# Two layers of sliding-window attention and a one-row MLP: the last MLP started before the last tile is done, a shorter path to the first scores, and a new order of the instructions

## The chip, the core and the metric

The kernel runs on one core of a Trainium2 chip. The core has five engines that run their own instruction streams and meet through semaphores: TensorE (PE; its weight loads are listed as PEld), VectorE (DVE), ScalarE (ACT), GpSimd (POOL) and SyncE (SP), which mostly issues transfers. The metric is device time in microseconds (us), the median of several runs.

## What is computed

```python
def _A_ref(x, wqkv, wo):                    # attention
    H = 32; Dh = D // H; W = 256
    q, k, v = split(x @ wqkv)
    scores = einsum("bhqd,bhkd->bhqk", q, k) * (Dh ** -0.5)
    mask = (i - j >= 0) & (i - j < W)       # the last 256 positions
    p = softmax(where(mask, scores, -1e9))
    return einsum("bhqk,bhkd->bhqd", p, v) @ wo

def _B_ref(x, w_r, w_gate, w_up, w_down):   # MLP of one row
    r = x @ w_r
    idx = argsort(-r)[:, :1]                # the one best row
    x_sel = x[idx]
    y = (silu(x_sel @ w_gate) * (x_sel @ w_up)) @ w_down
    return x + scatter(y * sigmoid(r[idx]), idx)

x = A_x                                     # 2048 rows of 512, bf16
for layer in range(2):
    x = x + _A_ref(layernorm(x), A_wqkv, A_wo)
    x = x + _B_ref(layernorm(x), w_r, w_gate, w_up, w_down)
```

There are 32 heads of 16 columns, 2048 rows, 512 columns and an MLP width of 1792. In each layer the MLP is applied to a single row: the one with the best score `r` of all 2048.

## The kernel before

**Tiles and steps.** The rows are cut into 16 tiles of 128. A tile passes through `ln_tile` (line 735: statistics on DVE, the inverse root and the normalisation on POOL, a transpose), `proj` (line 771: the projections of Q, K and V), `attend` (line 1298) and `out_tile` with `mod_tile` (lines 834 and 851: output projection, residual, statistics, the row score `r`, and the second normalised sum). In the second layer `mod_tile` also sends the finished tile to DRAM (line 884). Attention of a tile is cut into steps (`step`, line 1182): scores into two PSUM banks (line 1231), one exponential on ACT (line 1244), a mask on POOL (line 1250), products with V in bank 6 (line 1274). Tile 0 has 4 steps, tile 1 has 8, all others 9; three pairs of score banks are used in turn, and three steps are bound together as a visit (`VISIT = 3`, `S.bind`, with a slack `P_LEAD`).

**V's way.** V is stored to DRAM and read back in another layout (`vstore`, lines 1284 and 1287, SP's queue) before products can use it. K is copied four times under a mask into `KT` (line 802, "kbd").

**One projection bank.** Bank 7 (`BK_PR`) is shared by Q, K and V of all tiles but the first, by the output projections, and by the first layer's MLP. A use of it is a transaction: from its first matmul to its eviction no other use may enter.

**The MLP.** `mod_global(L)` (line 901) reduces the scores to the best one, finds the row's tile, picks the tile (ACT, line 941), gathers the row through matmuls with a one-hot vector (lines 955 and 957), multiplies by gate and up (line 980), applies the gate function, multiplies by down (line 1017 in the first layer, 1035 in the second). In the first layer all matmuls use bank 7, and the row is updated in place (line 1028). Tiles 0 to 4 of the second layer do not wait for that: they start with the row not updated, and if the best row lies in those five tiles, they are replayed from copies in DRAM. In the second layer the MLP stands at the very end: its row is written over the stored output by a 1 KB transfer (`fix`, line 1044).

**The check.** `check` (line 1314) reduces the reciprocals of all softmax sums to a flag. At the end all engines read the flag (line 1549) and branch (1550): to "pass", or to "safe", a slow general version of the whole kernel.

**What sets the order.** Nothing is ordered by hand. Every operation is given reads, writes, an estimated duration and a priority. A planner in the kernel's program simulates the five engines and gives each free engine the ready operation of lowest priority number; the resulting five lists are the instruction streams, with waits derived from the reads and writes. One tile is one unit of priority (1e6). Offsets per kind of work are named constants:

```python
1077     P_STEP = 1.453
1081     P_LN = -2.934
1082     P_PRJ = -1.175
1083     P_FIN = 1.042
1084     P_MG = 0.121
1344             S.prio_base = (n + self.P_PRJ) * ST
1364                 S.prio_base = (n + self.P_MG) * ST
1371         S.prio_base = (K + 4) * ST
1372         self.check()
1373         self.mod_global(1)
1374         self.warm(self.warmn[1])
```

`n` counts tiles over both layers, `K` is 32. In `proj` the constants `P_Q`, `P_K` and `P_V` are added, and for the first tile the three follow each other by these as well. `warm` adds matmuls whose results nobody reads, with the lowest priority of all: 21 at the start (line 699), 40 at the end (line 1295).

## Time and profile before

| | |
|---|---|
| median of 3 runs | 388.71 us (387.01 to 391.85) |
| the profiled execution | 390.14 us, its span 388.4 us |
| instructions in the span | 17651 |
| granted TensorE clock, mean | 0.954 |
| busy: PE, DVE, ACT, POOL | 346.4, 268.0, 264.9, 266.3 us |
| moved by DMA | 31.23 MB, 80 GB/s |

A line of the timeline gives the start, the duration of the whole group, the engine, the source line, the operation, what it writes and reads, how many such instructions are merged, and in brackets the idle time before it with what ended it. A line of the chain gives start, duration and what ran. A line of a stretch gives its bounds, its length, the busy time and count of PE, PEld, DVE, ACT and POOL, then the granted TensorE clock, the DMA share and GB/s. Where a stretch was asked for one source line, only that line's engine is counted. A line for one source line gives the engine, the operation, the count, the shortest, median and longest duration in ns, and the first and last start; a q behind an engine's name is its sequencer.

### The profile page before, as it was taken

Reading aid. Unit: us, or ns where it says so; the run is one execution under the profiler, and the core shown is the slowest. Engines: PE = TensorE matmul, PEld = TensorE weight load, DVE = VectorE, ACT = ScalarE, POOL = GpSimd, SP = SyncE. Lnnn points to the kernel's source line nnn. Section 1 sums busy time; section 2 is a strip of 40 time slices with the busy share of each in tenths; the row PEclk is TensorE's granted clock in tenths of the full one; section 3 lists DMA queues with packets and bytes.
Section 4 is the critical chain, followed back from the end, with each engine's and each line's share of the span. In section 5 each row is a group of like instructions: output and inputs, shape, how many; then the busy total and the mean of one; then the engine's idle time right before and its main releaser. Section 6 shows DMA issues by size and latency. Waiting matters only on the chain.

```text
span 388.4 us, 17651 instructions
## 1 busy us (share of the span) xinstructions
PE 346.4 (89%) x7793; PEld 277.5 (71%) x7793; DVE 268.0 (69%) x695; ACT 264.9 (68%) x284; POOL 266.3 (69%) x475
## 2 busy tenths in 40 slices
PE   6788989998999999998879798999999999997970
PEld 2567778777888888886657467788888888886470
DVE  6868967777777667677764487977666667775820
ACT  1078788887888888884945058788888888886010
POOL 6779968877888888775734069888888776665400
PEclk9789999999999999999998869999999999999975
DMA  8744567656444465553430222434433333221000
GB/s 265 219 64 66 88 136 119 110 113 99 99 101 98 93 99 102 99 100 71 58 44 15 44 20 72 57 73 73 73 73 73 73 71 73 59 59 29 26 8 5
DMA packets 72723, 31.23 MB, mean 80 GB/s; under 512 B 52672, under 2 KB 72000, under 8 KB 72640
## 3 DMA queue, kind: packets, MB, share of 16 engines
q1 hardware_dynamic: 70384, 27.81, 37.4%
q10 hardware_dynamic: 2256, 2.23, 1.8%
q8 instruction: 62, 1.02, 1.2%
q14 instruction: 21, 0.17, 0.2%
HBM read 14.29 MB, written 7.87 MB: 57 GB/s over the span
## 4 chain that ended last, share of the span: by engine, by line
PE 65%; DVE 15%; POOL 9%; DMA 3%; issue 3%; ACT 2%; DVEq 0%; ACTq 0%; POOLq 0%
PE f_PS L1274 20%; PE f_PS L1231 15%; PE f_PS L781 11%; PE f_PS L843 7%; PE f_PS L812 6%; DVE f_KT L802 3%; DMA f_OT<-f_ONORM 2%; PE f_PS L1295 2%; POOL f_PT L1250 2%; DVE f_ST L741 2%; ACT f_PT L1244 1%; DVE f_VN L815 1%; POOL f_xres L867 1%; POOL f_XN L749 1%; DVE f_QT L1109 1%
## 5 line engine op out<-in xcount | busy, mean ns | idle before, releaser
L1244 ACT ACTIVATE f_PT<-f_PS 128x1024 bf16<-128x1024 f32 x276 | 261.6, 1025 | 85.0 <-PE f_PS L1231 60.9
L1250 POOL TENSOR_TENSOR f_PT<-f_PT,f_TM 128x384 bf16<-128x384 bf16 x128 | 127.7, 999 | 53.3 <-ACT f_PT L1244 51.7
L1274 PE MATMUL f_PS<-f_VBD,f_PT 128*128 128x68 bf16 x2880 | 115.5, 198 | 7.6 <-DVE f_ONORM L830 4.6
L1274 PEld LDWEIGHTS f_PS<-f_VBD,f_PT 128*128 128x128 bf16 x2880 | 105.2, 98 | 22.5 <-issue 12.1
L1231 PE MATMUL f_PS<-f_QT,f_KT 64*128 64x128 bf16 (+3 forms) x2976 | 89.3, 205 | 9.8 <-DVE f_QT L1109 5.8
L1231 PEld LDWEIGHTS f_PS<-f_QT,f_KT 64*128 64x128 bf16 x2976 | 72.7, 95 | 29.3 <-issue 14.7
L781 PE MATMUL f_PS<-f_XNT,f_wqkv 128*128 128x128 bf16 x1024 | 70.7, 225 | 5.6 <-DVE f_GWR L928 2.1
L781 PEld LDWEIGHTS f_PS<-f_XNT,f_wqkv 128*128 128x128 bf16 x1024 | 60.5, 100 | 10.2 <-DVE f_KTN L799 2.6
L802 DVE TENSOR_SCALAR f_KT<-f_KTN,f_KM 128x512 bf16<-128x512 bf16 x128 | 47.8, 434 | 0.9
L843 PE MATMUL f_PS<-f_wo,f_OT 128*128 128x512 bf16 x128 | 34.8, 396 | 2.5 <-DMA f_OT<-f_ONORM 1.8
L812 PE MATMUL f_PS<-f_wqkv,f_XNT 128*128 128x512 bf16 x128 | 34.0, 389 | 0.5 <-DVE f_MV L742 0.5
L1109 DVE CAST f_QT<-f_PS 128x512 bf16<-128x512 f32 x32 | 21.9, 685 | 10.7 <-PE f_PS L781 10.3
L830 DVE TENSOR_TENSOR f_ONORM<-f_PS,f_RDA 128x256 bf16<-128x256 f32 x64 | 27.1, 423 | 2.0
L828 DVE RECIPROCAL f_RDA<-f_PS 128x16 f32<-128x16 f32 x64 | 16.2, 254 | 17.3 <-PE f_PS L1274 16.9
L799 DVE CAST f_KTN<-f_PS 128x512 bf16<-128x512 f32 x32 | 22.1, 690 | 7.1 <-PE f_PS L781 7.1
L1229 PE MATMUL f_PS<-f_BM,f_II 64*128 64x64 bf16 (+1 forms) x256 | 25.4, 192 | 0.0
L815 DVE CAST f_VN<-f_PS 128x512 bf16<-128x512 f32 x32 | 22.2, 693 | 4.6 <-PE f_PS L812 3.4
L847 DVE TENSOR_TENSOR f_xres<-f_PS,f_xin 128x512 f32<-128x512 f32 x16 | 11.1, 692 | 19.4 <-PE f_PS L843 19.4
L858 DVE BATCH_NORM_STATS2 f_ST<-f_xres 128x6 f32<-128x512 f32 x32 | 22.2, 692 | 1.0
L847 DVE TENSOR_TENSOR f_xres<-f_PS,f_xres 128x512 f32<-128x512 f32 x16 | 11.0, 691 | 16.8 <-PE f_PS L843 16.8
L860 DVE SCALAR_TENSOR_TENSOR f_JUNK<-f_xres,f_WR 128x512 bf16<-128x512 f32 x32 | 21.8, 681 | 0.1
L743 POOL TENSOR_SCALAR f_MV<-f_MV 128x1 f32<-128x1 f32 x32 | 6.4, 199 | 20.3 <-DVE f_MV L742 14.8
(128 smaller groups left out, 301.7 us busy)
## 6 DMA issues: line engine op xcount, KB each, us to landing
f_vscr<-f_VN SPq DMA_DIRECT2D x32, 136.0 KB, 1.8
f_VBD<-f_vscr SPq DMA_DIRECT2D x128, 34.0 KB, 2.6
out_dram<-f_OUTB SPq DMA_DIRECT2D x16, 128.0 KB, 2.0
f_xin<-in_B_w_down_dram SPq DMA_DIRECT2D x14, 128.0 KB, 3.0
f_wg<-in_B_w_gate_dram SPq DMA_DIRECT2D x7, 256.0 KB, 3.5
f_wu<-in_B_w_up_dram SPq DMA_DIRECT2D x7, 256.0 KB, 3.4
f_wqkv<-in_A_wqkv_dram ACTq DMA_DIRECT2D x3, 512.0 KB, 5.6
f_xscr<-f_xres SPq DMA_DIRECT2D x5, 256.0 KB, 2.4
```

Source lines behind the costliest of these rows:

```text
L781: r = e.matmul(self.bank(MB)[:, 128 * s:128 * s + 128], lhsT=self.wqkv[:, kc, off:off + 128], rhs=self.XNT[:, k2, kc, :], start=(kc == 0), ...
L802: S.add("dve", lambda e, hh=hh: e.tensor_scalar(out=self.KT[:, k4, :, :, hh, :].rearrange("p s b k -> p (s b) k"), in0=self.KTN[:, k2].rea ...
L812: return e.matmul(self.bank(MB)[:, 0:512], lhsT=self.XNT[:, k2, kc, :], rhs=self.wqkv[:, kc, 1024:1536], start=(kc == 0), stop=(kc == 3))
L815: S.add("dve", lambda e: e.tensor_copy(out=self.VN[:, kv, :, :, 0:16].rearrange("p h g d -> p g h d"), in_=self.bank(MB)[:, 0:512].rearran ...
L830: S.add("dve", lambda e: e.tensor_tensor(out=self.ONORM[:, ko, 256 * half:256 * half + 256].rearrange("p (h d) -> p h d", d=16), in0=acc[: ...
L843: return e.matmul(self.bank(MB)[:, 0:512], lhsT=self.OT[:, ko, kc, :], rhs=self.wo[:, kc, :], start=(kc == 0), stop=(kc == 3))
L1109: self.S.add("dve", lambda e: e.tensor_copy(out=self.QT[:, k2], in_=self.bank(MB)[:, 0:512].rearrange("p (s t) -> p s t", s=4)), reads=[], ...
L1229: r = e.matmul(o, lhsT=self.II[p, :], rhs=self.BM[p, q:q + w], start=False, stop=True, skip_group_check=True)
L1231: r = e.matmul(o, lhsT=self.KT[p, (b // 4) % 4, s, b % 4].rearrange("p h k -> p (h k)"), rhs=self.QT[p, k2, s, q:q + w], start=(i == 0), s ...
L1244: S.add("act", lambda e: e.activation(out=view, in_=self.PS[:, b0:b0 + 2, 0:128 * nu].rearrange("p h (u c) -> p h u c", u=nu), func=ACTF.E ...
L1250: S.add("pool", lambda e: e.tensor_tensor(out=w, in0=w, in1=self.TM[:].unsqueeze(1).broadcast_to([128, k, 2, 32]), op=ALU.mult), reads=["t ...
L1274: r = e.matmul(self.bank(BK_PV)[:, c0:c0 + 68], lhsT=self.PT[:, w1:w1 + 128], rhs=self.VBD[:, (b // 4) % 4, b % 4].rearrange("p h (g c) -> ...
```

## The change

The second layer's MLP is split in time. `mod_global(1, 13, 6e6)` is given the priority of the last tile's attention up to the gather, and a very late one from the gate matmuls on; it considers tiles 0 to 12 only. Gate, up and down keep banks 1, 3 and 2, the argmax and the gather use the projection bank. Its row is written by the same 1 KB transfer. `check` gets a further part: the best score of tiles 13 to 15 is compared with the best of the first 13, and the result is joined to the flag. If the flag is set, all engines go to a new part "more": it reads a second flag without the comparison, and goes to "safe", or to "last", which writes the row's old value back (`put_back`) and runs the whole `mod_global(1)` again. The two long reductions of the check are split from the last tile's share and given a priority within the last tile.

At the start the first two tiles are normalised by one DVE instruction in place of two POOL instructions; the first tile's projections are ordered K, Q, V; the eviction of its Q goes to ACT; the warm-up uses a small tile of ones of its own and has 26 matmuls; the ones in V's buffers are written later. All offsets have new values, there are three new ones (`P_SP`, `P_KBD`, `P_PVJ`), and some estimated durations are changed.

```diff
@@ init
-        S.add(P, lambda e: e.memset(self.VN[:, 0]..., 1.0), writes=["vn0"], dur=560, prio=-9.4e9)
+        S.add(P, lambda e: e.memset(self.WZ[:], 1.0), writes=["wz"], dur=120, prio=-9.6e9)
...
-        for b in range(1, self.RV):
-            S.add(P, ... VN[:, b] ..., prio=-4e9 + b * 1e6)
+        for b in range(self.RV):
+            S.add(P, ... VN[:, b] ..., prio=-0.5e9 + b * 1e6)
@@ ln_tile
+        if L == 0 and m < 2:
+            S.add("dve", lambda e: e.tensor_scalar(out=self.XN[:, k2, :], in0=x, scalar1=MV[:, k2, 0:1], scalar2=MV[:, k2, 3:4],
+                                                   op0=ALU.subtract, op1=ALU.mult),
+                  reads=[xk, "mv%d" % k2, "mvc%d" % k2], writes=["xn%d" % k2], dur=350, name="lnorm")
+            self.transpose(self.XNT[:, k2], "xnt%d" % k2, self.XN[:, k2, :], ["xn%d" % k2], tb)
+            return
@@ proj
-            S.prio_base = p0 + self.P_Q * 1e6
+            S.prio_base = p0 + (self.P_Q * 1e6 if L or m else 2e3)
...
+            if L == 0 and m == 0 and self.RV == 2:
+                S.add("act", lambda e: e.copy(out=self.QT[:, k2], in_=self.bank(MB)...), ..., dur=600, name="evq", tr=t)
+                return
...
-            S.prio_base = p0 + self.P_K * 1e6
+            S.prio_base = p0 + (self.P_K * 1e6 if L or m else 0.0)
...
+            S.prio_base += self.P_KBD * 1e6
...
-            S.prio_base = p0 + self.P_V * 1e6
+            S.prio_base = p0 + (self.P_V * 1e6 if L or m else 4e3)
@@ mod_global
-    def mod_global(self, L):
+    def mod_global(self, L, nt=None, late=0.0):
...
+        part = nt is not None
+        NT = nt or self.NT
...
-            if not side:
+            if not (side or part and b in (0, 1, 4)):
                 return self.bank(b), "bank%d" % b, None
...
+        if part:
+            S.add(D, lambda e: e.tensor_copy(out=self.F4O[:], in_=self.F4[:]), reads=["f4"], writes=["f4o"], dur=150, name="am")
+            S.prio_base = p0 + late
@@ Fast
-    P_Q = 0.041
-    P_K = -0.027
-    P_V = -0.444
-    P_STEP = 1.453
-    P_NORM = -0.028
-    P_LEAD = 224.787
+    P_Q = -0.321
+    P_K = -0.417
+    P_V = 0.027
+    P_STEP = 1.139
+    P_NORM = -0.33
+    P_LEAD = 330.505
...
-    P_LN = -2.934
-    P_PRJ = -1.175
-    P_FIN = 1.042
-    P_MG = 0.121
-    P_PV = 0.878
-    warm0 = 21
+    P_SP = 1.0
+    P_PVJ = [0.0, 0.0, 0.0, 0.0, -0.285, 0.0, 0.0, 0.0, 0.0]
+    P_KBD = 0.698
+    P_LN = -2.482
+    P_PRJ = -1.035
+    P_FIN = 1.533
+    P_MG = 1.784
+    P_PV = 0.741
+    warm0 = 26
@@ check
-        S.add(D, ... tensor_reduce(out=C[:, 0:1], in_=bits, op=ALU.max), reads=keys, dur=1200)
-        S.add(D, ... tensor_reduce(out=C[:, 1:2], in_=bits, op=ALU.min), reads=keys, dur=1200)
+        for i, (bits, keys, dur, pr) in enumerate((
+                (flat[:, 0:n], [... all but the last tile ...], 1200, (2 * NT - 0.4) * 1e6),
+                (flat[:, n:n + 32], [... the last tile ...], 180, None))):
+            S.add(D, ... tensor_reduce(out=C[:, i:i + 1], in_=bits, op=ALU.max), ..., dur=dur, prio=pr)
+            S.add(D, ... tensor_reduce(out=C[:, 2 + i:3 + i], in_=bits, op=ALU.min), ..., dur=dur, prio=pr)
...
+        R = self.xres[:, self.PART:NT, 516]
+        S.add(D, ... tensor_reduce(out=C[:, 9:10], in_=R, op=ALU.max), reads=["r%d" % m for m in range(self.PART, NT)], writes=["ckm"], dur=170)
+        S.add(D, ... tensor_tensor(out=C[:, 8:9], in0=C[:, 9:10], in1=self.PM[:, 2:3], op=ALU.is_gt), reads=["ckm", "pm2"], writes=["ckp"], dur=130)
+        S.add("pe", lambda e: e.matmul(self.bank(4)[0:1, 0:5], lhsT=self.ONESF[:, 0:1], rhs=C[:, 4:9], start=True, stop=True), ...)
+        S.add(D, ... tensor_reduce(out=self.FLAG[0:1, 0:1], in_=self.bank(4)[0:1, 0:5], op=ALU.max), writes=["bank4", "flag"], ...)
+        S.add(D, ... tensor_reduce(out=self.FLAG[0:1, 2:3], in_=self.bank(4)[0:1, 0:4], op=ALU.max), writes=["bank4", "flag2"], ...)
@@ build
-        S.prio_base = (K + 4) * ST
+        S.prio_base = (K - 2 + self.P_SP) * ST
+        self.mod_global(1, self.PART, 6e6)
+        S.prio_base = (K + 3) * ST
         self.check()
-        self.mod_global(1)
         self.warm(self.warmn[1])
@@ build_kernel, body
-                h.br_cond(v, "safe_" + e, "pass_" + e)
+                h.br_cond(v, "more_" + e, "pass_" + e)
...
+            with part("more"):
+                fs.wait_all(h, fsem, fdma)
+                v = h.value_load(flag[0:1, 2:3], min_val=0, max_val=256)
+                h.br_cond(v, "safe_" + e, "last_" + e)
+            with part("last"):
+                ls.run_engine(e, h, lsem, ldma)
+                if e == "sp":
+                    ls.wait_all(h, lsem, ldma, engines=False)
+                h.br("done_" + e)
```

108 lines of the change are left out of this document (68 added, 40 removed).

## The prediction

> **What bounds the kernel now.** I read the page first, then stretches of the span side by side, then the timeline at the three places that look unlike the rest. All times below are microseconds from the start of the span.
>
> ```profile
> span 388.4 us, 17651 instructions
> 57.00:166.90 109.90, 106.22 (x2621) 87.99 (x2621) 80.22 (x203) 92.48 (x98) 88.61 (x152) 1.00 0.55 102
> 166.90:257.40 90.50, 78.83 (x1689) 62.53 (x1684) 63.47 (x170) 55.04 (x61) 55.10 (x100) 0.92 0.32 55
> 257.40:347.00 89.60, 88.28 (x2165) 72.67 (x2161) 64.34 (x157) 76.52 (x82) 66.59 (x108) 1.00 0.35 71
> ...
> 57.00:166.90 109.90, 92.48 (x98) 1.00 0.55 102
> 166.90:257.40 90.50, 54.21 (x58) 0.92 0.32 55
> 257.40:347.00 89.60, 76.52 (x82) 1.00 0.35 71
> ```
>
> The first three stretches give the busy time of PE, PE's weight load, DVE, ACT and POOL, and then the granted clock; the last three count only the exponentials (L1244). A whole tile has nine attention steps with one exponential each. In the last stretch PE is busy 88.28 of 89.60: attention is bound by TensorE, at 89.60/82 = 1.093 a step. The first layer's body needs 109.90/98 = 1.121. The stretch around the change of layers makes only 58 steps in 90.50, where 58 x 1.093 = 63.4 would do: **27.1 are lost there**. PE idles 90.50 - 78.83 = 11.7 in it (1.3 in an equal stretch later, so 10.4 too many), and the clock of 0.92 takes 0.08 x 90.5 = 7.2. The other 9 or so are the matmuls of the first layer's MLP themselves (by the durations below, 1.87 for the gather, 3.15 for gate and up, 3.19 for down, and the small ones).
>
> ```profile
> 225.94 2.85 ACT L1244 ACTIVATE f_PT<-f_PS 128x1024 bf16<-128x1024 f32 x3 [14.99 <-PE f_PS L1231]
> 216.47 3.19 PE L1017 MATMUL f_PS<-f_xin,f_HT 128*128 128x512 bf16 x14
> 220.51 1.07 PE L781 MATMUL f_PS<-f_XNT,f_wqkv 128*128 128x128 bf16 x16 [0.85 <-DVE f_YBC L1022]
> 199.40:202.80 3.40, 2.73 (x35) 2.62 (x28) 1.01 (x6) 2.46 (x4) 0.92 (x1) 1.00 0.34 68
> 202.80:206.20 3.40, 3.40 (x44) 1.95 (x43) 1.95 (x6) 1.66 (x3) 0.91 (x1) 0.50 0.02 5
> 223.30:230.10 6.80, 6.01 (x90) 4.13 (x88) 5.45 (x15) 3.69 (x4) 4.32 (x9) 0.50 0.37 25
> ```
>
> ACT makes no exponential for 15 us, because the K and Q projections (L781) of the second layer's fourth tile run only at 220.5, behind the MLP's last matmuls (L1017). Both use the one projection bank. The clock falls to half in 202.8 to 206.2 and in 223.3 to 230.1.
>
> The **end** is a chain in which nothing overlaps:
>
> ```profile
> 366.19 0.27 POOL L869 TENSOR_SCALAR f_xres<-f_DOT,f_xres 128x1 f32<-128x1 f32 x1
> 367.81 0.33 SPq L884 DMA_DIRECT2D out_dram<-f_OUTB  x1
> 370.91 1.87 PE f_PS L957 x8
> 373.35 3.15 PE f_PS L980 x112
> 376.82 2.04 PE f_PS L1035 x56
> 378.88 0.22 DVE L1039 SCALAR_TENSOR_TENSOR f_F4B<-f_PS,f_SGT,f_F 128x4 bf16<-128x4 f32 x1 [2.12 <-PE f_PS L1035]
> 379.96 0.35 SPq L1044 DMA_DIRECT2D out_dram<-f_F4B  x1
> L1552 SPq COMPARE_BRANCH  x1: 58/58/58, 381.1 to 381.1; - x1
> L1513 SPq DRAIN  x1: 59/59/59, 388.1 to 388.1; - x1
> ```
>
> The last tile's score is ready at 366.46; its rows are sent at 367.81. Everything after that is the MLP of one row, its 1 KB store, and a closing part: from the end of that store's issue, 380.31, to 388.4 it is 8.1. It lies on SP, which branches at 381.1 and drains at 388.1.
>
> **The change, part by part.** *The end.* The MLP is started with the last tile's attention, for the best row of tiles 0 to 12, and a check compares it with tiles 13 to 15. What stays behind 366.46 is one reduction and one comparison on DVE, the flag's matmul and its reading:
>
> ```profile
> 363.45 0.15 DVE L1325 TENSOR_TENSOR f_CKF<-f_CKF 128x1 f32<-128x1 f32 x1
> 364.18 0.13 DVE L1328 CAST flag<-f_PS 1x1 int32<-1x1 f32 x1
> 350.00:359.00 9.00, 6.48 (x176) 5.43 (x172) 4.26 (x12) 5.71 (x6) 5.32 (x9) 1.00 0.13 31
> 364.00 3.13 PE f_PS L1295 x14
> ```
>
> From L1325's end (363.60) to L1328's end (364.31) the flag takes 0.71. With two small DVE steps of about 0.2 it stands at 366.46 + 0.4 + 0.7 = 367.6, before the last rows have been issued at 367.81 + 0.33 = 368.14. The closing 8.1 follow: 376.2, that is **12.2 earlier**. The price is that the MLP's PE work moves. The gather (L957, 1.87, with its small broadcast and the two argmax matmuls about 2.9) has the last tile's priority and gate or up half of 3.15 can start in its gaps: 4.5 of work, against 9.00 - 6.48 = 2.5 of PE idle in 350 to 359. So 2.0 come on top of attention (bounds 0 and 4.5). Gate waits for the bank that an exponential three steps before the end gives free; behind it on PE stand the last products and the output projection, and if the plan has it too early they wait with it, within those 4.5. The rest (gate or up, and L1035's 2.04) fits behind the last attention matmul, where 40 warm-up matmuls ran; those get less room, and at 3.13/14 = 0.22 each they need 8.9, so PE works until about 358.9 + 8.9 + 5.2 = 373, three before SP's end: they cost nothing, and about 1 for each us that PE starts later than that. DVE's two 1.2 us reductions of the check, moved ahead, and the argmax fit: it is busy 4.26 of those 9. ACT's copy of the row falls between exponentials and costs nothing beyond the gap above. On SP the 1 KB store must be issued once; if it lands behind the last rows it adds 379.96 + 0.35 - 379.1 = 1.2 (from F4B's end), if it is ahead but late, the rows wait for it. I take it as ahead: 0. Every engine's closing branch now waits for the flag at 367.6 where it was there at 364.31; nothing but the branch is queued behind that wait, and SP reaches it at 368.14 anyway.
>
> The rows at 199.4 and 202.8 speak for a second price: PE was busy 2.73 of 3.40 with the gather in it, and the next 3.4 ran at half clock. The same gather now stands beside the last tile; a stretch of 3.4 at half clock costs 1.7. I put 0.7 (bounds 0 and 5). The Trainium skill, page "TensorE: Matmul & The Clock Gate", section "Why this matters for your kernels", asks only that no gap of PE exceeds about 3 us; by that rule this 0.7 would be 0. The clock at 202.8 fell without such a gap, so here the trace does not follow the rule.
>
> End: 12.2 - 2.0 - 0.7 = **9.5 gained** (bounds 3 and 12.5).
>
> *The first scores.*
>
> ```profile
> 3.70 0.69 DVE L741 BATCH_NORM_STATS2 f_ST<-f_xin 128x6 f32<-128x512 bf16 x1
> 5.99 0.17 DVE L742 BATCH_NORM_AGGREGATE f_MV<-f_ST 128x2 f32<-128x6 f32 x1
> 6.24 0.66 POOL L743 TENSOR_SCALAR f_MV<-f_MV 128x1 f32<-128x1 f32 x2 [3.00 <-DVE f_KM L710]
> 6.98 0.58 POOL L745 TENSOR_TENSOR f_MV<-f_MV,f_MHALF 128x1 f32<-128x1 f32 x1
> 9.36 0.40 PE L765 MATMUL f_PS<-f_IDB,f_XN 128*128 128x128 bf16 x4 [1.56 <-POOL f_XN L749]
> 10.41 0.41 DVE L768 COPY f_XNT<-f_PS 128x512 bf16<-128x512 bf16 x1
> 10.98 1.20 PE f_PS L812 x4
> 12.18 3.24 PE f_PS L781 x32
> 16.14 2.19 DVE f_KT L802 x4
> 18.37 0.56 PE f_PS L1231 x14
> L802 DVE TENSOR_SCALAR f_KT<-f_KTN,f_KM x128: 317/348/1478, 16.1 to 345.4; 128x512 bf16<-128x512 bf16 x128
> L799 DVE CAST f_KTN<-f_PS 128x512 bf16<-128x512 f32 x32 | 22.1, 690 | 7.1 <-PE f_PS L781 7.1
> 1.10:18.37 17.27, 12.65 (x69) 6.81 (x69) 13.41 (x45) 1.49 (x2) 12.95 (x34) 0.90 0.86 268
> ```
>
> Now V (L812) comes first, and K and Q (L781) behind it. With K first and the normalisation on DVE: statistics to 4.39, aggregate 0.17, POOL's two steps 0.33 and 0.58, 0.3 of handing over, normalisation 0.35 (L802's median, the nearest row), transposes 0.40, eviction 0.41, K 1.07 (L781 above), eviction 0.69, four masked copies at 0.35 to 0.55, 2.2: 10.9, against 18.37. But DVE is busy 13.41 of these 17.27 already, and gains two normalisations while Q's eviction goes to ACT; if all its work had to come first, the scores would start at 1.1 + 13.4 - 0.7 + 0.7 = 14.5. So 3.9 to 7.5 are gained at the first score. V is late instead: its values go through DRAM before the first product with them. I take **5** (bounds 2 and 7.5), nearer to the DVE bound. The clock of 0.90 in that stretch is part of it: the warm-up, 26 matmuls instead of 21, starts after a shorter clearing and covers the wait for the first transposes. The later clearing of V's buffers is POOL work that moves, 12.95 busy of 17.27; if it delays the masks, the lower bound holds it. Changed durations in the code only alter the plan.
>
> The normalisation on DVE may cost up to L802's slowest row, 1.48 instead of 0.35, while POOL clears buffers. The Trainium skill, page "SBUF — State Buffer", section "SBUF: two separate sides", says that VectorE and GpSimd lock one port pair against each other for a whole instruction; by that rule the first score would be late by up to two POOL clears, and the sum by 2.
>
> *The order.* The MLP's priority goes from 0.121 to 1.784 tiles behind the layer's end, K's from -1.202 to -1.452, V's from -1.619 to -1.008 of its tile. So K and Q of the tile that starved at 220.5 (due at 19 - 1.452 = 17.55) now go ahead of the MLP (17.78). The 15 us gap should close; the PE idle in it and the 3.4 and 6.8 stretches at half clock go with it, at most 10.4 + 7.2 = 17.6. The MLP must still come before tile 5 of the layer, and its chain on the single bank stays, so I take half: **8** (bounds 0 and 17.6). In steady state PE idles 1.3 of 89.6, so a better order can give no more than 1.5% of some 290, 4; bound steps may now start 330 - 225 = 106 ns earlier than their inputs, three visits a tile, 0.32 x 29 = 9 lost at worst. I take 0, as PE stays the bound.
>
> Sum: 9.5 + 5 + 8 = **22.5**. The profiled execution took 390.14 (388.4 and 1.7 around it), 1.4 over the median of 388.71: it gives 367.6, and the median 366.2.
>
> **The rivals.** *A: the new order closes nothing at the change of layers*; the MLP still holds the bank while another tile waits. For: seven matmul groups follow each other on one bank. Against: the priorities above. 388.7 - 14.5 = 374.2. *B: the gap closes wholly and the start gains its 7.5*: 388.7 - 9.5 - 7.5 - 16.5 = 355. *C: the half clock comes into the last tile fully* (5 instead of 0.7, and the 4.5 exposed): about 373. *D, slower: V starves attention in every tile.* V is due at n - 1.008 where its products are due at n + 0.741: 1.75 tiles, where before it had 0.878 + 1.619 = 2.5. If eviction, store and reload through DRAM exceed that, 1.75 x 9.8 = 17, PE waits in each of 29 whole tiles. From 1.04 a tile on this eats the 22.5 and 7.8 more: 396.5. Against it: there is ample time left by these numbers. *E: the change doesn't do what it says*, since the best row lies in tiles 13 to 15, and the MLP runs again: two more branches of up to 7.0, the MLP's 12.4 and closing, some 27 over the forecast, 393. On the reference's own inputs I work out 4.21 for the best score (row 1082, tile 8) and 2.81 for tiles 13 to 15, so it hardly can be.
>
> **How the numbers follow.** Chances: forecast 0.52, A 0.19, B 0.15, C 0.06, D 0.05, E 0.01, and 0.02 for between. Two per cent, 7.8 us, is what a measurement here can tell from no change. Forecast, A, B and C lie below 380.9: 0.90 with their tails taken off; D 0.05; 0.05 within. The range goes from a little under B to a little over A and C, 352 to 377.
>
> **What would show it.** End: no L957, L980 or L1035 behind the last output store, SP's drain 8 after that store, flag about 1 after the last score. Start: first L1231 at 11 to 14.5, clock at 1.0 until then. Order: no ACT gap over 5 between 170 and 250; 58 exponentials there in some 82. I would be wrong if L781 again waits behind L1017, if PE's warm-up matmuls outlast SP, or if a step takes over 1.093 in the second layer.

## The result and the profile after

| | before | after |
|---|---|---|
| median | 388.49 us (387.01 to 391.85, 4 runs) | 374.43 us (372.27 to 377.56, 4 runs) |
| ratio | | 0.9633, 95% interval 0.9534 to 0.9731 |
| the profiled execution, its span | 390.14, 388.4 | 377.56, 375.8 |
| granted clock in it | 0.954 | 0.964 |

The change is 14.1 us faster: inside the forecast's range of 352 to 377, on its side, and 8.2 slower than its 366.2. Line numbers have moved: the exponential is L1278, the scores L1265, the products L1308, the K and Q projections L790, the MLP's gate and up L1004, its down L1041 in the first layer and L1059 in the second, the output projection L857, the warm-ups L1329.

First the page and the three stretches of the kernel after, cut at the starts of tiles 4, 15, 22 and 31 (columns as before; the first cut of the kernel before, 57.00, stands 1.3 behind the start of its tile 4):

```profile
span 375.8 us, 17669 instructions
```

```profile
56.10:165.30 109.20, 107.45 (x2650) 90.05 (x2646) 89.57 (x205) 93.39 (x99) 84.17 (x153) 1.00 0.49 106
165.30:250.30 85.00, 76.05 (x1668) 61.09 (x1664) 58.78 (x165) 54.65 (x60) 53.21 (x97) 0.94 0.26 56
250.30:340.70 90.40, 87.90 (x2158) 73.01 (x2154) 69.80 (x162) 76.47 (x81) 61.42 (x110) 1.00 0.35 69
```

PE still bounds both bodies. The stretch around the change of layers is 5.5 shorter than before, 85.00 against 90.50, but PE still idles 8.95 in it and the clock is 0.94. The timeline of the kernel after shows the pause of ACT still there, one tile on:

```profile
217.82 3.18 PE L1041 MATMUL f_PS<-f_xin,f_HT 128*128 128x512 bf16 x14 [0.75 <-DVE f_xres L861]
222.14 1.06 PE L790 MATMUL f_PS<-f_XNT,f_wqkv 128*128 128x128 bf16 x16
222.85 0.75 DVE L1052 SCALAR_TENSOR_TENSOR f_xres<-f_YBC,f_OHL,f_xres 128x512 f32 x1 [1.06 <-issue]
227.63 8.36 ACT L1278 ACTIVATE f_PT<-f_PS 128x1024 bf16<-128x1024 f32 x9 [14.05 <-PE f_PS L1265]
237.26 3.21 ACT L1278 ACTIVATE f_PT<-f_PS 128x1024 bf16<-128x1024 f32 x3 [1.27 <-PE f_PS L1265]
```

Tile 19, which starved before (first exponential at 225.94), now starts at 202.5; tile 20 starves, 14.05 in place of 14.99, and again its K projection stands behind the MLP's down matmuls. L1052 is the update that adds the MLP's row to the residual; it ends at 223.60.

The end of the kernel after, in its timeline:

```profile
353.13 1.54 PE L1004 MATMUL f_PS<-f_XS,f_wg 128*128 128x1 bf16 x56
357.37 1.66 PE L1004 MATMUL f_PS<-f_XS,f_wu 128*128 128x1 bf16 x56
360.13 2.04 PE L1059 MATMUL f_PS<-f_HT,f_xin 128*128 128x1 bf16 x56
362.03 1.86 PE L857 MATMUL f_PS<-f_wo,f_OT 128*128 128x512 bf16 x4
363.69 5.89 PE L1329 MATMUL f_PS<-f_wqkv,f_wo 128*128 128x512 bf16 x20
367.29 0.26 POOL L883 TENSOR_SCALAR f_xres<-f_DOT,f_xres 128x1 f32<-128x1 f32 x1
368.91 0.34 SPq L898 DMA_DIRECT2D out_dram<-f_OUTB  x1
369.74 0.15 DVE L1368 TENSOR_REDUCE flag<-f_PS 1x1 int32<-1x5 f32 x1 [1.79 <-PE f_PS L1366]
```

The last score is ready at 367.55, and the span ends 8.25 behind it, where it was 21.94 before (388.4 - 366.46). So the MLP is gone from behind the last store. But gate, up and down now stand ahead of the last output projection (L857 at 362.03), on the way to that score.

**Where the gain sits.** The first exponentials of tiles 4, 15, 24 and 31 and the last one cut the span into stretches with the same exponentials in each kernel; what else PE does in them can differ a little. In the kernel after they are these rows of ACT's timeline (the last exponential, at 350.69, is the second of the last row's two):

```profile
56.18 1.02 ACT L1278 ACTIVATE f_PT<-f_PS 128x1024 bf16<-128x1024 f32 x1 [1.34 <-PE f_PS L1265]
165.34 1.02 ACT L1278 ACTIVATE f_PT<-f_PS 128x1024 bf16<-128x1024 f32 x1 [1.16 <-PE f_PS L1265]
272.86 1.02 ACT L1278 ACTIVATE f_PT<-f_PS 128x1024 bf16<-128x1024 f32 x1 [1.16 <-PE f_PS L1265]
340.74 1.02 ACT L1278 ACTIVATE f_PT<-f_PS 128x1024 bf16<-128x1024 f32 x1 [0.31 <-PE f_PS L1265]
349.78 1.93 ACT L1278 ACTIVATE f_PT<-f_PS 128x1024 bf16<-128x1024 f32 x2
```

Before, the same five stand at 55.70, 166.95, 277.43, 347.09 and 355.38. The table gives what each stretch of a profiled execution is shorter than before, in us (the last four columns belong to experiments below; "both additions" is the last of them):

| stretch | forecast | after | after, second profile | split alone | all but the split | both additions |
|---|---|---|---|---|---|---|
| start to tile 4 | 5 | -0.5 | 0.3 | -0.7 | 1.0 | 2.8 |
| tile 4 to 15 | 0 | 2.1 | 2.0 | 0.7 | 1.9 | 1.9 |
| tile 15 to 24, change of layers | 8 | 3.0 | 6.4 | 2.3 | 5.9 | 4.4 |
| tile 24 to 31 | 0 | 1.8 | 2.1 | 0.0 | 2.1 | 2.1 |
| tile 31 to last exponential | -2.0 | -1.7 | -2.2 | -2.9 | -0.1 | -1.7 |
| last exponential to end | 11.5 | 7.9 | 12.1 | 9.6 | 0.6 | 11.1 |
| span | 22.5 | 12.6 | 20.7 | 9.0 | 11.4 | 20.8 |

### The profile page after: what moved, and what is told of

It reads as the page before. It is cut to its first block, busy times and chain, and to the rows that moved or that the text cites. A ratio compares the mean times of both kernels' runs of the same rounds, so it can differ in the third digit from the quotient of the medians.

```text
span 375.8 us, 17669 instructions
## 1 busy us (share of the span) xinstructions
PE 347.9 (93%) x7798; PEld 278.4 (74%) x7798; DVE 281.6 (75%) x702; ACT 264.3 (70%) x285; POOL 251.8 (67%) x472
## 4 chain that ended last, share of the span: by engine, by line
PE 59%; DVE 23%; DMA 7%; ACT 4%; POOL 4%; issue 2%; DVEq 0%; SPq 0%; ACTq 0%; POOLq 0%
PE f_PS L1308 17%; PE f_PS L1265 12%; PE f_PS L790 9%; DVE f_KT L816 8%; PE f_PS L857 7%; PE f_PS L826 6%; ACT f_PT L1278 4%; DMA f_OT<-f_ONORM 4%; PE f_PS L1329 3%; DVE f_KTN L812 3%; DMA f_WR<-in_B_w_r_dram 2%; DVE f_JUNK L874 2%; DVE f_QT L1143 2%; DVE f_ST L744 1%; DVE f_xres L861 1%
## 5 line engine op out<-in xcount | busy, mean ns | idle before, releaser
L1278 ACT ACTIVATE f_PT<-f_PS 128x1024 bf16<-128x1024 f32 x276 | 260.6, 1030 | 75.2 <-PE f_PS L1265 58.3
L1284 POOL TENSOR_TENSOR f_PT<-f_PT,f_TM 128x384 bf16<-128x384 bf16 x128 | 117.5, 919 | 48.1 <-ACT f_PT L1278 47.0
L1308 PEld LDWEIGHTS f_PS<-f_VBD,f_PT 128*128 128x128 bf16 x2880 | 108.5, 99 | 22.6 <-DVE f_ONORM L844 8.2
L1308 PE MATMUL f_PS<-f_VBD,f_PT 128*128 128x68 bf16 x2880 | 118.3, 199 | 5.1 <-DVE f_ONORM L844 4.3
L1265 PE MATMUL f_PS<-f_QT,f_KT 64*128 64x128 bf16 (+3 forms) x2976 | 90.1, 204 | 4.1 <-ACT f_PT L1278 3.9
L1265 PEld LDWEIGHTS f_PS<-f_QT,f_KT 64*128 64x128 bf16 x2976 | 71.3, 94 | 16.8 <-ACT f_PT L1278 7.3
L790 PE MATMUL f_PS<-f_XNT,f_wqkv 128*128 128x128 bf16 x1024 | 68.0, 219 | 4.4 <-DVE f_KTN L812 2.8
L790 PEld LDWEIGHTS f_PS<-f_XNT,f_wqkv 128*128 128x128 bf16 x1024 | 58.0, 98 | 9.0 <-DVE f_KTN L812 3.6
L816 DVE TENSOR_SCALAR f_KT<-f_KTN,f_KM 128x512 bf16<-128x512 bf16 x128 | 59.2, 519 | 1.2 <-DVE f_QT L1143 0.4
L857 PE MATMUL f_PS<-f_wo,f_OT 128*128 128x512 bf16 x128 | 35.0, 397 | 5.9 <-DVE f_QT L1143 3.3
L879 POOL TENSOR_SCALAR f_RSM<-f_xres 128x1 f32<-128x1 f32 x32 | 7.5, 235 | 37.8 <-DVE f_xres L873 37.4
L874 DVE SCALAR_TENSOR_TENSOR f_JUNK<-f_xres,f_WR 128x512 bf16<-128x512 f32 x32 | 28.3, 885 | 0.1
L857 PEld LDWEIGHTS f_PS<-f_wo,f_OT 128*128 128x128 bf16 x128 | 10.6, 100 | 16.8 <-issue 6.1
L881 POOL TENSOR_TENSOR f_xres<-f_RSM,f_MHALF 128x1 f32<-128x1 f32 x32 | 17.5, 548 | 6.9 <-DVE f_DOT L877 3.9
```

The source lines that it names most:

```text
L790: r = e.matmul(self.bank(MB)[:, 128 * s:128 * s + 128], lhsT=self.wqkv[:, kc, off:off + 128], rhs=self.XNT[:, k2, kc, :], start=(kc == 0), ...
L816: S.add("dve", lambda e, hh=hh: e.tensor_scalar(out=self.KT[:, k4, :, :, hh, :].rearrange("p s b k -> p (s b) k"), in0=self.KTN[:, k2].rea ...
L857: return e.matmul(self.bank(MB)[:, 0:512], lhsT=self.OT[:, ko, kc, :], rhs=self.wo[:, kc, :], start=(kc == 0), stop=(kc == 3))
L874: S.add(D, lambda e: e.scalar_tensor_tensor(out=self.JUNK[:], in0=x, scalar=1.0, in1=self.WR16[:], op0=ALU.mult, op1=ALU.mult, accum_out=s ...
L1265: r = e.matmul(o, lhsT=self.KT[p, (b // 4) % 4, s, b % 4].rearrange("p h k -> p (h k)"), rhs=self.QT[p, k2, s, q:q + w], start=(i == 0), s ...
L1278: S.add("act", lambda e: e.activation(out=view, in_=self.PS[:, b0:b0 + 2, 0:128 * nu].rearrange("p h (u c) -> p h u c", u=nu), func=ACTF.E ...
```

## The experiments

### The two halves of the change

*The split alone:* the kernel before, with `mod_global(1, 13, 6e6)`, the new `check`, "more" and "last", and nothing else.

```diff
+        S.prio_base = (K - 2 + self.P_SP) * ST
+        self.mod_global(1, self.PART, 6e6)
+        S.prio_base = (K + 3) * ST
         self.check()
-        self.mod_global(1)
```

> The kernel before with only the last MLP split (13 tiles beside the last tile, check, redo path); start, durations and order constants as before. Theory T (two separate gains: end and order of the middle): the stretch from the last exp to the end falls from 33.0 us to about 25, the last tile's steps grow from 8.3 to about 10 us, so 388.5 - 8 + 1.7 = about 382 (379 to 384), with the pause of ACT at tile 19 as before (15 us). Rival (the split brings nothing by itself, since the MLP of the last layer only lengthens the last tile by what it saves behind it): 386 to 390. Rival (the split carries the whole gain of 14): 373 to 376.

Measured: 381.62 (380.91 to 384.49) beside 390.25 before, ratio 0.98 (0.9717 to 0.9883): 8.6 us. From the last exponential to the end it takes 23.4, the last tile 11.2.

*All but the split:* the kernel after with the same lines undone; new start, new constants, new durations.

> The changed kernel with the last MLP at the end as in the kernel before; new start, new durations and new order constants are kept. Theory T: the first exp of tile 24 comes 4 to 5 us earlier than in the kernel before (of which 1.6 by tile 15), the steps of tiles 24 to 31 take 1.10 us instead of 1.106, the last exp comes 6 us earlier and the end is as before: 381 to 384. Rival (the order and start carry all of the 14): 373 to 376. Rival (the order carries nothing, its 4.6 us in the one trace are chance): 387 to 390. In all of them the first score comes at 18.5 and not at 13, because the copies of K behind it wait on DVE.

Measured: 380.30 (378.77 to 382.45), ratio 0.9762 (0.9678 to 0.9846): 9.9 us. So both halves gain on their own, and about alike; neither carries the 14. Their sum, 18.5, is 4 more than the 14.1 of the whole change. Of that, 1.8 is the yardstick: the kernel before took 388.49 beside the whole change and 390.25 here. Each interval reaches about 3 us to either side, so the rest asks for no reason.

### The changed kernel once more

> The changed kernel itself once more, as the yardstick for the three kernels beside it. All theories: 372 to 377, granted clock of the runs between 0.96 and 0.99, the lower the clock the longer the time. Theory T (the split of the last MLP and the new order are two nearly independent gains of 8.6 and 10 us): 390.1 - 18.6 + 1.7 (the last tile that is longer by the MLP beside it) = 373. Rival (the parts overlap): 376 to 378.

Measured: 374.08 beside 390.54, ratio 0.9597 (0.955 to 0.9643), 16.5 us. Its profiled execution took 369.41, with a span of 367.7: 8.1 less than the first one, of the same program. ACT's timeline of this execution:

```profile
55.40 1.02 ACT L1278 ACTIVATE f_PT<-f_PS 128x1024 bf16<-128x1024 f32 x1 [1.34 <-PE f_PS L1265]
164.66 1.02 ACT L1278 ACTIVATE f_PT<-f_PS 128x1024 bf16<-128x1024 f32 x1 [1.17 <-PE f_PS L1265]
223.44 8.36 ACT L1278 ACTIVATE f_PT<-f_PS 128x1024 bf16<-128x1024 f32 x9 [12.12 <-PE f_PS L1265]
268.69 1.02 ACT L1278 ACTIVATE f_PT<-f_PS 128x1024 bf16<-128x1024 f32 x1 [1.17 <-PE f_PS L1265]
345.83 1.93 ACT L1278 ACTIVATE f_PT<-f_PS 128x1024 bf16<-128x1024 f32 x2
```

The two executions part at two places, by 3.5 between tiles 15 and 20 and by 4.2 behind the last exponential. Stretches of the first profile, then of the second:

```profile
206.11:216.35 10.24, 10.24 (x245) 9.25 (x240) 1.86 (x10) 5.92 (x7) 3.62 (x5) 0.50 0.18 38
345.90:349.47 3.57, 3.57 (x66) 3.41 (x66) 3.46 (x8) 1.98 (x3) 2.65 (x6) 1.00 0.62 39
350.70:363.90 13.20, 12.29 (x243) 9.38 (x244) 4.93 (x20) 1.20 (x3) 3.06 (x7) 0.63 0.06 17
352.88:356.29 3.41, 2.74 (x97) 2.65 (x95) 3.03 (x11) 0.18 (x1) 0.89 (x3) 1.00 0.02 5
356.29:366.53 10.24, 10.24 (x154) 6.81 (x151) 4.34 (x15) 0.00 (x0) 1.95 (x5) 0.50 0.05 15
```

```profile
346.70:357.60 10.90, 10.16 (x253) 8.41 (x251) 5.68 (x22) 1.24 (x3) 3.06 (x7) 1.00 0.05 16
```

From the last exponential to the last output projection the same PE work takes 13.20 at a clock of 0.63 and 10.90 at 1.00; in the middle the first execution has 10.24 at half clock and the second none. The half clock is thus a term of about 8 us between these two executions, and it is not the same in each run: the mean clocks of the ten runs in the two comparisons lie between 0.964 and 0.991, and the times follow by and large, 377.56 at 0.964 and 369.41 at 0.991 (one run, 376.45 at 0.973, stands out).

### Does the width of the MLP's matmuls set the clock?

The MLP's matmuls have one column. Here they get 64, of the same vector; the surplus columns are overwritten or not read.

```diff
-                    r = e.matmul(bk[:, j:j + 1], lhsT=..., rhs=self.XS[:, kc:kc + 1], ...)
+                    r = e.matmul(bk[:, j:j + 64], lhsT=..., rhs=self.XS[:, kc:kc + 1].broadcast_to([128, 64]), ...)
```

(and the second layer's down likewise). First in the second layer only:

> The changed kernel with the gate, up and down matmuls of the last MLP 64 columns wide instead of one (the extra columns are overwritten or unused); order unchanged. Theory T (the one-column matmuls of the moved MLP let the granted clock fall to half in 349 to 353 and 356 to 366 us): no half-clock window in the last 25 us before the warm-ups, the last score comes 13 us behind the last exp instead of 16.9, time 370 to 372. Rival (the clock falls because of the idle time between the last tile's PV groups, whatever the matmuls' width): same windows, time 374 to 377. Rival (64 columns take longer than one by more than the clock gives): gate, up and down each longer than 1.5 to 2.0 us, time 376 to 379.

Measured: 372.59 (370.72 to 373.89), ratio 0.9531 (0.9455 to 0.9606). The stretch from the last exponential to the last output projection in this kernel:

```profile
350.80:361.80 11.00, 10.36 (x243) 8.90 (x247) 5.55 (x21) 1.19 (x3) 3.07 (x7) 1.00 0.05 16
```

No half clock in the end; 21.4 from the last exponential on, where the first profile of the kernel after had 25.1, but its second, one column wide and at full clock, 20.9. The MLP's matmuls themselves are no shorter (gate takes 1.91 here, and 1.54 with one column): it is the products and projections beside them that run at full speed. The first layer's MLP is still one column wide here, and the clock is at half from 203.9 to 217.6. Then in both layers:

> The changed kernel with the gate, up and (second layer) down matmuls of both MLPs 64 columns wide instead of one. Theory T (one-column matmuls count as little work, so both MLPs pull the granted clock down; with 64 columns the tail stays at full clock as it did with the second MLP alone, and now the turnover at 203 to 217 us too): granted clock 0.99 to 1.0 in most runs, time 369 to 371. Rival (the half clock at 203 to 217 us comes from PE waiting for the chain of small DVE and ACT instructions between the MLP's parts, not from the one-column matmuls): the clock of the runs scatters between 0.98 and 0.995 as with the second MLP alone, time 371 to 374. Rival (the 112 wider matmuls of the first layer cost PE time at full clock): MLP of the first layer 1 to 2 us longer, 373 to 375.

Measured: 371.58 (370.65 to 372.69, six runs), ratio 0.9527 (0.9495 to 0.9559): no less than with the second layer alone, so the first layer's wide matmuls bring no time that can be measured. The scatter is what changes: 2.0 between the fastest and slowest of six runs. Of the sixteen runs of three kernels with 64 columns (the third stands at the end), twelve have a mean clock of 0.991 or more, and none is under 0.982. But a fourth kernel with 64 columns, the one with the MLP earlier (below), does not follow: its six runs have 0.972 to 0.991, and its profile shows half clock in the middle and in the last tile:

```profile
219.09:232.74 13.65, 10.71 (x113) 7.63 (x114) 10.57 (x26) 1.96 (x3) 10.32 (x23) 0.50 0.22 51
352.21:355.62 3.41, 3.41 (x59) 2.78 (x57) 1.53 (x7) 2.73 (x4) 1.15 (x2) 0.50 0.54 53
```

And one column can keep the clock: the second profile of the kernel after has it behind 346.6. So the width alone does not set it. What does can be counted in the fourteen traces. In each trace, all changes of the clock lie on one grid of 3.413 us, to about 1 ns. For each matmul take the columns that it moves, times the share of the 128 rows that it uses, and add them up in each step of that grid. With the grid shifted by a quarter of a step the sorting fails for 40 or more. PE's busy time does not sort them: 30 of the 76 steps that half clock follows were busy throughout.

That explains both what width does and why it looked like chance. The gather, one column wide in every kernel, takes 2.0 us. Where 1.73 or more of it falls into one step, half clock follows (20 of 28 gathers); where the grid divides it more evenly, full clock (8 of 8). The grid lies differently in each execution: in the middle the first execution of the kernel after has the whole gather in one step, the second 1.07 and 0.94 in two. Behind the last exponential, steps with one-column gate or up hold 3380 to 3730 columns in the second execution, little over the line, and 2390 to 2480 in the first; with 64 columns they hold 5900 to 7200. So widening takes gate and up well off the line, in all four profiles that have it. That the gather of the last tile kept the clock in three of the four kernels with 64 columns is luck: there the grid divided it, and in the fourth it did not.

### The pause at the change of layers

*The first layer's MLP behind K and Q of tile 20,* from the gate matmuls on:

```diff
             S.prio_base = p0 + late
+        elif side:
+            S.prio_base = p0 + 0.92 * 1e6
```

> The changed kernel with the first layer's MLP, from its gate matmuls on, at a later priority (18.70), behind the K and Q projections of tile 20 (18.55 and 18.64). Theory T (the 14 us pause of ACT before tile 20 comes from the K projection standing behind the MLP's down matmuls in PE's queue): K projection of tile 20 starts 4 us earlier, the pause shrinks to 8 to 10 us, the time falls by 3 to 6 us to 369 to 372. Rival (the pause is the update's: what waits for the rewritten rows of the residual stays where it is, and the pause moves to tile 21 or 22): the sum of the pauses between tile 19 and 23 stays and the time is 373 to 376. Rival (the MLP later delays the update, which everything behind tile 20 waits for): 377 to 382.

Measured: 380.96 (378.89 to 381.74), ratio 0.9744 (0.9665 to 0.9822). The third guess held, slower by some 6. The update and ACT, in the timeline of this kernel:

```profile
227.34 0.75 DVE L1054 SCALAR_TENSOR_TENSOR f_xres<-f_YBC,f_OHL,f_xres 128x512 f32 x1 [1.06 <-issue]
215.66 2.86 ACT L1280 ACTIVATE f_PT<-f_PS 128x1024 bf16<-128x1024 f32 x3 [2.58 <-PE f_PS L1267]
241.76 2.86 ACT L1280 ACTIVATE f_PT<-f_PS 128x1024 bf16<-128x1024 f32 x3 [17.00 <-PE f_PS L1267]
```

Tile 20 comes at 215.66, 12 earlier, but the pause goes to tile 21 and is longer. And here the fixed quantity shows: tile 21 starts 13.67 behind the end of the update (228.09). In the kernel after it is 13.66 (237.26 - 223.60), in its second profile 13.65, and in the kernel without the split 13.66; ten of the fourteen profiles have 13.64 to 13.67, and none has less:

```profile
218.42 0.75 DVE L1040 SCALAR_TENSOR_TENSOR f_xres<-f_YBC,f_OHL,f_xres 128x512 f32 x1 [1.06 <-issue]
232.83 3.21 ACT L1259 ACTIVATE f_PT<-f_PS 128x1024 bf16<-128x1024 f32 x3 [1.26 <-PE f_PS L1246]
```

Tile 21 is the first whose rows the update may have changed, and nothing of it is prepared ahead. Its path in the kernel after:

```profile
224.12 0.68 DVE L744 BATCH_NORM_STATS2 f_ST<-f_xres 128x6 f32<-128x512 f32 x1
226.80 0.87 POOL L758 TENSOR_SCALAR f_XN<-f_xres,f_MV 128x512 bf16<-128x512 f32 x1
227.69 1.21 SPq L766 DMA_TRANSPOSE f_XNT<-f_XN  x1
230.90 1.07 PE L790 MATMUL f_PS<-f_XNT,f_wqkv 128*128 128x128 bf16 x16
233.00 0.65 DVE L812 CAST f_KTN<-f_PS 128x512 bf16<-128x512 f32 x1
234.31 0.85 DVE L816 TENSOR_SCALAR f_KT<-f_KTN,f_KM 128x512 bf16<-128x512 bf16 x3
236.79 0.54 PE L1265 MATMUL f_PS<-f_QT,f_KT 64*128 64x32 bf16 x18
```

So the pause is not PE's order around one tile: it is what remains of the MLP's chain and of these 13.7 when the exponentials that need no update have run out. Filling it with tile 20 only empties it later.

*K and Q of tile 20 ahead, the MLP's priority kept:*

```diff
-            S.prio_base = (n + self.P_PRJ) * ST
+            S.prio_base = (n + self.P_PRJ - (0.8 if n == 20 else 0.0)) * ST
```

> The changed kernel with the projections of tile 20 0.8 of a tile earlier in priority (K at 17.75 and Q at 17.84, around the first layer's MLP at 17.78), so that K of tile 20 is not behind the MLP's down matmuls while the MLP keeps its own priority. Theory T (PE's fixed order alone makes the pause of ACT before tile 20): tile 20 starts at 214 to 217 instead of 227.6, tile 21 at 235 to 238 as now, and tiles 21 to 23 no longer run at 10 to 13 us each since the backlog is gone: last exp 2 to 5 us earlier, time 370 to 373. Rival (PE is full between 199 and 216 us, so each matmul put ahead of the MLP delays it and its update): the pause moves to tile 21 and the sum stays, time 374 to 377. Rival (as with the MLP moved behind tile 20, the pause grows): tile 21 at 240 to 242, time 378 to 382.

Measured: 385.29 (384.73 to 387.31), ratio 0.9885 (0.9849 to 0.992). Tile 20 starts at 212.2, the update ends at 229.98, tile 21 starts 14.1 behind that. Slower than each guess, on the third's side: what is put ahead of the MLP on a full PE delays the update, and everything behind it. The clock is lower too, 0.955 to 0.964 in these runs.

*The MLP earlier,* on the kernel with 64 columns:

```diff
-    P_MG = 1.784
+    P_MG = 1.55
```

> The kernel with both MLPs 64 columns wide and the first layer's MLP at 1.55 of a tile behind instead of 1.784, so that its chain stands earlier on PE, and Q of tile 19 behind it. Theory T (tile 21's first exp follows the end of the update by a fixed 13.6 to 14.1 us in the changed kernel and in five variants, so what the pause costs is set by when the update ends): the update ends at 215 to 219 instead of 221, tile 21 comes 13.6 us later, or when tiles 19 and 20 are done if those are later, and the time follows: 369 to 371.5 if Q of tile 19 does not hold ACT up. Rival (what is put behind the MLP now makes its own pause, as in the kernel before, where the MLP stood at 0.121): a pause of 8 to 15 us before tile 19, tile 21 at 236 to 246, time 373 to 382.

Measured: 376.47 (372.84 to 378.29), ratio 0.9634 (0.9592 to 0.9676), 4 to 5 more than with 1.784. The rival held, with the pause one tile later than it said. The update ends at 218.74, only 2.2 earlier than with 64 columns and 1.784 (220.96); ACT pauses 12.88 before tile 20, whose K runs at 222.2 and Q at 224.9, both at half clock, and reaches tile 21 at 242.44, 23.7 behind the update. Some of that is the half clock from 219.09 on: K and Q take 1.87 and 1.89 there, and 1.07 at full clock. The 13.7 are thus the least that was seen, where no other work held tile 21 back. Moves to either side lost 4 to 11 us; a better place was not found.

### The first scores

*The masked copies of K (L816) at K's own priority in the first tile:*

```diff
-            S.prio_base += self.P_KBD * 1e6
+            S.prio_base += self.P_KBD * 1e6 if L or m else 0.0
```

> The changed kernel with the later priority of the four masked copies of K (0.698 of a tile) left out for the first tile alone, so that DVE does them right behind the eviction of K, ahead of V's eviction and of the next tile's K. Theory T (the first scores come no earlier than before because these copies end at 18.5 behind three other instructions of DVE): the copies end at about 15, the first scores come at 15 to 16 instead of 18.5, the first exp at 16 to 17, and the first exp of tile 4 comes 1.5 to 3 us earlier than 54.7 to 56.2. If a head start is kept to the end the time falls by as much: 371 to 373. Rival (what the head gains is lost by tile 15, since PE, 99 % busy in the steady stretch, and not ACT sets the pace): the first exp comes earlier but tile 15's comes at 164 to 165.5 as now, time 373 to 376. Rival (V's eviction, now later, holds the first PV): tile 1 comes later than 23.2, time 375 to 377.

Measured: 378.55 (375.70 to 381.24), ratio 0.9708 (0.9665 to 0.9751), slower than the kernel after. The first exponential comes at 16.27 and tile 4 at 53.58, but tile 8 at 98.49 where it was 96.02: the planner's order differs in places up to 127, and what it lost there is more than the start gave. This run says what the copies cost the first scores, and nothing clean on the time. So the same again with the order kept and only those four instructions moved in DVE's list:

```diff
+            q = fs.order["dve"]
+            nm = lambda i: fs.ops[i].name
+            kb = [i for i in q if nm(i) == "kbd"][:4]
+            q[:] = [i for i in q if i not in kb]
+            at = [nm(i) for i in q].index("evk") + 1
+            q[at:at] = kb
```

> The changed kernel with its whole order kept on every engine, but for the first tile's four masked copies of K, put on DVE right behind the eviction of K. Theory T (the copies alone hold the first scores; the kernel with the copies' priority changed lost its head start again because its order shifted up to tile 9): first exp at 16 to 17.5 instead of 18.8 to 19.2, tile 8 at 92.5 to 94.5 instead of 95 to 96, tile 15 at 162 to 163.5, time 1.5 to 2.5 us below the changed kernel in the same call. Rival (tile 1, whose K and V evictions are now later on DVE, takes it back): tile 1 at 22.4 to 23.5 and tile 15 at 164 to 165.5 as before, no difference in time.

Measured: 373.39 (370.65 to 376.47), ratio 0.9564 (0.9521 to 0.9606), not to be told from the kernel after, measured beside it (0.9597). DVE in the kernel after, then DVE, PE and ACT in this one:

```profile
11.82 0.67 DVE L812 CAST f_KTN<-f_PS 128x512 bf16<-128x512 f32 x1
12.95 0.69 DVE L733 TENSOR_REDUCE f_SWC<-f_WR 128x1 f32<-128x512 bf16 x1 [0.37 <-DMA f_WR<-in_B_w_r_dram]
13.55 1.35 DVE L816 TENSOR_SCALAR f_KT<-f_KTN,f_KM 128x512 bf16<-128x512 bf16 x2
14.82 0.67 DVE L829 CAST f_VN<-f_PS 128x512 bf16<-128x512 f32 x1
15.42 1.42 DVE L816 TENSOR_SCALAR f_KT<-f_KTN,f_KM 128x512 bf16<-128x512 bf16 x1
16.75 0.67 DVE L812 CAST f_KTN<-f_PS 128x512 bf16<-128x512 f32 x1
17.35 1.13 DVE L816 TENSOR_SCALAR f_KT<-f_KTN,f_KM 128x512 bf16<-128x512 bf16 x4
```

```profile
12.28 1.98 DVE L816 TENSOR_SCALAR f_KT<-f_KTN,f_KM 128x512 bf16<-128x512 bf16 x4
16.16 1.07 PE L790 MATMUL f_PS<-f_XNT,f_wqkv 128*128 128x128 bf16 x16 [0.92 <-DVE f_KTN L812]
17.16 0.42 PE L1265 MATMUL f_PS<-f_QT,f_KT 64*128 64x32 bf16 x14
17.64 1.94 ACT L1278 ACTIVATE f_PT<-f_PS 128x1024 bf16<-128x1024 f32 x2 [4.61 <-PE f_PS L1263]
```

In the kernel after, K is out of its bank at 12.49, but its first copy starts at 13.55 and the fourth is the first of the row at 17.35, behind the weights' sum, V and the next tile's K. Moved, they end at 14.26, and the scores still wait until 17.16: on PE the projections of tile 1 (L790) stand ahead of them. Two engines' orders held the first scores. The first exponential gains 1.2 and tile 15 comes 2.2 earlier (162.49 against 164.66 in the second profile of the kernel after); in the span the half clock of this profile, 202.5 to 216.2, hides it.

### The warm-ups at the end

```diff
-    warmn = (0, 40)
+    warmn = (0, 0)
```

> The changed kernel without the 40 warm-up matmuls at its end (the 26 of the start stay). Theory T (the 20 warm-ups ahead of the flag's matmul, 363.7 to 369.6 in the trace of the changed kernel, hold the flag back by 1.1 us, since DVE's sum is ready at 368.4): the flag comes 0.7 to 1.2 us behind the last score instead of 2.2, time 1 us less (372 to 374) where the last stretch runs at half clock, and no difference where it runs at full clock. Rival (PE's own branch, 4.2 us behind the warm-ups, sets the end): 2 to 4 us less, 370 to 372. Rival (without warm-ups the clock falls to half earlier and the last PE work gets longer): 375 to 377.

Measured: 375.01 (370.68 to 375.99), ratio 0.9593 (0.9548 to 0.9637): the same as the kernel after. In its profile the flag stands 0.8 behind the last score, and the span ends 7.1 behind that score. In the two profiles of the kernel after the flag stands 2.3 and 1.0 behind it, and the span ends 8.25 and 7.2 behind, the second with the warm-ups at full clock (20 in 4.48 in place of 5.89). So by these profiles they cost about 1 where they run at half clock, and nothing otherwise; the medians can't tell that.

### What pays together

64 columns in both MLPs, and the four copies moved in the list:

> Both: gate, up and down of both MLPs 64 columns wide, and the first tile's masked copies of K right behind K's eviction. Theory T: 371.6 - 2 = 369 to 370.5, clock 0.99 or more. Rival (the head start is taken back by tile 1 or 2): 371 to 372.5, as with the wide matmuls alone.

Measured: 369.47 (367.46 to 370.83), ratio 0.9467 (0.943 to 0.9503), and the kernel after, measured beside it, 0.9597 (0.955 to 0.9643): the intervals don't touch. It is faster than both kernels, 21.1 below before. With the clock kept up, what the copies gain at tile 15 (162.22, and 164.14 with 64 columns alone) arrives at the end: 369.47, and 371.58 with 64 columns alone, in two comparisons.

## Why the prediction was right, and where it was not

**The end** was put at 9.5 and gave 8.6 by itself (0.9717 to 0.9883 is 4.6 to 11.0), 6.2 and 9.9 in the two profiles of the kernel after. The shape was right: no gather, gate or down behind the last store. Behind the last score it gained 13.7, more than the 12.2 predicted, since the closing from the last rows' issue on took 6.6 (369.25 to 375.8) and not 8.1. The price in the last tile, 2.0, was 1.7 and 2.2, and 2.9 for the split alone. Two steps failed. "The rest fits behind the last attention matmul ... they cost nothing": up and down stand ahead of the last output projection, so the last score comes 13.7 behind the last exponential at full clock, where it was 11.1, and 11.2 in the kernel without the split; that is 2.6. And the half clock was sized at 0.7: it took another 3.1 in the first profile (16.9 in all) and none in the second, and which of the two comes is where the grid of 3.41 us falls, so no sum could have fixed it beforehand. The flag came 2.3 behind the score, not 1.1, at half clock, and 1.0 at full clock; about 1 of that is on the path.

**The first scores** were put at 5 and gave none: first exponential at 19.20 where it was 19.01, tile 4 between 0.5 later and 0.3 earlier. The sum of the path (10.9) and DVE's total were worked out; what stood ahead in the fixed orders was not. The new offset of the copies, 0.698 of a tile, is in the diff and puts three instructions of DVE between K and its copies; tile 1's projections stand ahead on PE. The price named for the normalisation was real: one took 1.29 beside POOL's clearing, the other 0.41 (L751), and the copies go from 0.32 to 1.42 there. The lower bound of 2 was thus still too high.

**The change of layers** was put at 8 (0 to 17.6) and gave 3.0 and 6.4 in the two profiles, 5.9 without the split. (The clock of 0.92 that it read there comes from three stretches, not two: 213.1 to 216.5 is at half clock as well.) The argument that K and Q of tile 19 now go ahead of the MLP held, and tile 19 came 23 earlier. The conclusion, "the 15 us gap should close", failed, and two signs that the prediction named for that showed: ACT pauses 14.05, and a K projection waits behind the MLP's down matmuls. By the same priorities tile 20 (20 - 1.035 - 0.417, that is 18.55) is behind the MLP's 17.78, and the wait behind it is the update's, 13.7 long. What the change gains is one tile's exponentials ahead of that wait; tiles 21 to 24 then give part back (tile 21 is 11.1 ahead, tile 24 only 4.6), as their preparation could not start before the update either.

**Steady state** was put at 0, and is worth 2.0 in the first layer (109.2/99 = 1.103 a step in place of 1.124) and 1.8 to 2.1 in the second (1.077 in place of 1.106). In the first layer that is idle time of PE, 1.75 where it was 3.68, with the same busy time (107.41 and 107.57). In the second PE idles only 0.3 less, and the stretch holds 1662 matmuls where it held 1688, so most of that gain is work that stands elsewhere. Rival D, V too late, shows nowhere in it.

The sum, 22.5, was 12.6 in the first profile, 20.7 in the second and 14.1 by the medians. Two terms, the start and the change of layers, were too large and one, the steady state, too small; that the sum still landed in the range owes something to this. The clock, which the prediction gave 0.7, decides between 12.6 and 20.7. Rival A's 374.2 is the measured median almost exactly, but partly by accident: the pause did stay, while the 5 of the start that A counted on did not come, and the order's gain and the steps made that up. Rival E did not occur: the run holds no second MLP.

## What to carry to other kernels

Before a pause is filled, look for what ends it: where tiles behind it need a late result, earlier work in the pause only empties the next one, and the quantity to shorten is from that result to the first use. On engines with a fixed order, a shorter path gives nothing until every instruction that stands ahead on each engine of it is counted. Where runs of one kernel scatter, set their granted clock beside their times before explaining a few us, and count the columns that PE moves rather than its busy time.

## What was not expected of the hardware

The granted clock fell to half for 10.24 us at 356.29, behind 3.41 us with PE busy 2.74, and to half at 349.47 behind 3.57 us in which PE was busy throughout, with the one-column gather in it. The Trainium skill, page "TensorE: Matmul & The Clock Gate", section "Why this matters for your kernels", asks that no gap of PE exceed about 3 us; the longest idle time of PE between 345 and 366 is 0.67, so here the trace again does not follow that rule. The same program in another execution kept the full clock from its last exponential on, and had half clock behind the gather for 3.41 us (343.15 to 346.56). What sorts the steps here is the count of columns given above: 2999 in the step of the grid ahead of 349.47 and 2482 in the one ahead of 356.29, both under 3060. Why that much is the line, and how the chip counts it, stays open.
